# Half of wo and the FFN modulation weights in one transfer ahead of the last K, the other half behind the last V

## The chip, the cores and the metric

The kernel runs on one core of a Trainium2 chip. The metric is device time in microseconds (us), the median of a few runs. The profile is of one such execution; its span is the time from the first instruction to the last.

## The reference

One block of a decoder, for one token of each of 4 sequences: adaptive layer norm, attention over a cached window of 2048 positions with grouped heads, and a gated FFN. All data are fp32.

```python
mod = (_silu(c) @ w_mod).reshape(c.shape[0], 6, 1, -1)
sa, ca, ga, sb, cb, gb = (mod[:, 0], mod[:, 1], ..., mod[:, 5])
h = _layernorm(x, axis=-1) * (1 + ca) + sa
x = x + ga * _A_ref(h, A_k_cache, A_v_cache, A_wq, A_wo)   # attention, then @ wo
h = _layernorm(x, axis=-1) * (1 + cb) + sb
x = x + gb * _B_ref(h, B_w1, B_w3, B_w2)                   # (silu(h @ w1) * (h @ w3)) @ w2
return x
```

x is 4 x 512, there are 32 query heads on 8 key heads of 128 each, w_mod is 512 x 3072, wq 512 x 4096, wo 4096 x 512, w1 and w3 512 x 1792, w2 1792 x 512. Keys and values are by far the largest part: 8 MB for each of the 8 key heads (4 MB of K, 4 MB of V; MB and KB are powers of two wherever sizes of transfers are told, as in the profile's KB).

## The kernel before

**Memory.** One SBUF tensor, `ring`, holds three slots of 8 MB (64 KB on each of the 128 partitions); `HALF` is half a slot. Every large input is brought into a slot by a transfer that SP issues, in program order on one queue: `load(dst, src)` is one such transfer. In order: the attention part of w_mod (`w_mod_a`), x and c, wq, then K and V of groups 0 to 6 as one transfer of 8 MB each (`kv_in`), wo (8 MB), K of group 7 and V of group 7 apart (4 MB each), `w_mod_b` (the four FFN and gate parts of w_mod, 4 MB, with w1, 3.5 MB, in one transfer), w3 (3.5 MB), and w2 in four pieces (`W2_CUTS`: 8, 4, 1 and 1 fourteenths of 3.5 MB). In the profile all pieces of w1, w2 and w3 that have a transfer of their own are called `w`.

**Order.** The class `Program` records every operation in the order written, works out from the regions that operations touch which must wait for which, and puts a semaphore wait ahead of an instruction where its engine does not know already that the other is done. A transfer into a slot waits for the last matmul that reads what it overwrites. Each engine, SP among them, keeps the written order. Since all operations are issued in one helper line, all rows of the profile have the same line, and instructions are told apart by their tiles.

**Stages.** After the first norm, the query projection and the transposed queries (`qT`), `group(g)` runs for each of the 8 key heads: scores (`s_ps<-ring,qT`, 16 matmuls), the maximum on DVE (`mx`), the exponential on ACT (`p_sb`), transposed probabilities (`bank<-ident,p_sb`, then `pT`), and the product with V (`o_ps<-ring,pT`). ACT then scales the output into `o_sb`. `heads_out(g)` transposes it with the matrix `pick` into `oT`; it is called inside the next group, and for the last group after it. `project_out(g)` adds the product of this group's output and its rows of wo to `a_ps` (4 matmuls of width 512, tile `a_ps<-ring,oT`). Each fp32 matmul of the program gives two records in the trace.

wo arrives only between K of group 6 and K of group 7, so `project_out` is called for groups 0 to 5 just ahead of group 7, and for 6 and 7 after it. Then come `work` (a copy of `a_ps`), the product with `spread` that lays the attention output out over partitions (`attn`), `mod_columns` (16 matmuls `bank<-ring,sc` of width 512, from the activated c in `sc` and the FFN part of w_mod, copied to `mod_b`), the residual `x1`, the second norm, its transposition `h2T`, `ffn_in` for the gate (w1) and for up (w3) (`s_ps<-ring,h2T`), the hidden vector `hidT`, and the product with w2 (`s_ps<-ring,hidT`, 56 matmuls of width 128), gate, residual and the output.

Of the kernel before, what the change touches and what calls it, by code (L numbers as in the profile page):

```python
# [8 lines left out]
B, D, HQ, G, SK, DH, W, FF = 4, 512, 32, 8, 8192, 128, 2048, 1792  # L9
P = 128  # L10
R = HQ // G
# [1 line left out]
NC = 4  # L13
CHUNKS = [(c, j) for c in range(4) for j in range(4 if c < 2 else 3)]
NF = len(CHUNKS)
W2_CUTS = [0, 8, 12, 13, 14]
EPS = 1e-5
HALF = 8192

# [118 lines left out]
                nc.sync.sem_clear(done)  # L138


def block_kernel(nc, xc_in, w_mod_a, wq, kv_in, wo, w_mod_b, w3, w2, out):

# [1 line left out]
    do = Program(nc)  # L146

    def sb(name, *shape):
        return nc.alloc_sbuf_tensor(name, (P, *shape), F32).ap()

    def ps(name):
        return nc.alloc_psum_tensor(name, (P, 512), F32).ap()

    ring = sb("ring", 6 * HALF)
    slots = [ring[:, n * 2 * HALF : (n + 1) * 2 * HALF] for n in range(3)]
    s_ps = [ps(f"s_ps{t}") for t in range(NT)]
    banks = [ps(f"bank{n}") for n in range(2)]
    a_ps, o_ps = ps("a_ps"), ps("o_ps")
    turn = [0]

    def bank():
        turn[0] += 1
        return banks[turn[0] % 2]

    def load(dst, src):
        do("sync", "dma_start", dst, src)
        return dst

    def batch(t):

# [4 lines left out]
    x_sb, ct_sb = xc_sb[:, :P], xc_sb[:, P:]  # L175


    wma = load(slots[0][:, : w_mod_a.shape[1]], w_mod_a)
    load(xc_sb, xc_in)
    wq_t = load(slots[1], wq)  # L180
    kv = [None] * G
    kv[0] = load(slots[2], kv_in[0])
# [27 lines left out]
    oT = sb("oT", G, R, B)  # L210
# [9 lines left out]
    ss, ln, r0, ve, a, r = (sb(n, 1) for n in ("ss", "ln", "r0", "ve", "a", "r"))  # L220
# [26 lines left out]
    def mod_columns(wv, dst, n):  # L247

        pb = bank()
        for k in range(4):  # L250
            for j in range(4):
                do("tensor", "matmul", pb[32 * j : 32 * j + 32, : n * P], sc[:, k, :], wv[:, k, j, :], start=(k == 0), stop=(k == 3))
        do("vector", "tensor_copy", dst, pb[:, : n * P])
# [21 lines left out]
    for half in range(2):  # L275
# [4 lines left out]
        for i in range(R):  # L280
            src = qtp[:, i * P : (i + 1) * P].rearrange("p (g q) -> p g q", g=4)[:, :, ::8]
# [7 lines left out]

    def project_out(g):  # L290
        for i in range(R):
            do("tensor", "matmul", a_ps[32 * i : 32 * i + B, :], oT[:, g, i, :], wo_t[:, g, i, :], start=(g == 0), stop=(g == G - 1))

    mx, nm, ls, l, rl = (sb(n, m) for n, m in (("mx", NT), ("nm", 1), ("ls", NT), ("l", 1), ("rl", 1)))
    p_sb = [sb(f"p_sb{t}", 512) for t in range(NT)]
# [3 lines left out]
    def heads_out(g):  # L299

        otp = bank()[:, : R * B]
        for c in range(NC):
            do("tensor", "matmul", otp, o_sb[:, c * P : (c + 1) * P], pick[:, c].rearrange("p r b -> p (r b)"), start=(c == 0), stop=(c == NC - 1))
        do("vector", "tensor_copy", oT[:, g].rearrange("p r b -> p (r b)"), otp)

    def group(g):
        kt, vt = (kv[g][:, i * HALF : (i + 1) * HALF].rearrange("p (t b n) -> p t b n", t=NT, b=B) for i in range(2))
        for t in range(NT):
            for b in range(B):
                do("tensor", "matmul", s_ps[t][32 * b : 32 * b + 32, :], qT[:, g, b, :], kt[:, t, b, :], start=True, stop=True)  # L310
            do("vector", "reduce_max", mx[:, t : t + 1], s_ps[t], axis=AX.X)
        do("vector", "tensor_reduce", nm, mx, axis=AX.X, op=ALU.max, negate=True)
        if g:
            heads_out(g - 1)
        for t in range(NT):
            do("scalar", "activation", p_sb[t], s_ps[t], AF.Exp, bias=nm, accum_out=ls[:, t : t + 1])
            pt = bank()
            for c in range(NC):
                do("tensor", "transpose", pt[:, c * P : (c + 1) * P], p_sb[t][:, c * P : (c + 1) * P], ident)
            do("vector", "tensor_copy", pT[t], pt.rearrange("p (c b i) -> p b c i", b=B, i=32)[:, :, :, :R])  # L320
            for u in [t - 1] * (t > 0) + [t] * (t == NT - 1):
                for b in range(B):
                    do("tensor", "matmul", o_ps[32 * b : 32 * b + NC * R, :], pT[u][:, b].rearrange("p c r -> p (c r)"), vt[:, u, b, :], start=(u == 0), stop=(u == NT - 1))
        do("vector", "reduce_sum", l, ls, axis=AX.X)
        do("vector", "reciprocal", rl, l)
        do("scalar", "activation", o_sb, o_ps, AF.Copy, scale=rl)

    for g in range(G - 1):
        group(g)
        if g < 4:  # L330
            kv[g + 3] = load(slots[(g + 2) % 3], kv_in[g + 3])
        elif g == 4:
            wo_t = load(slots[0], wo).rearrange("p (g r n) -> p g r n", g=G, r=R)
        elif g == 5:
            kv[7] = slots[1]
            for i in range(2):
                load(kv[7][:, i * HALF : (i + 1) * HALF], kv_in[7][:, i * HALF : (i + 1) * HALF])
    wmb = load(slots[2][:, : w_mod_b.shape[1]], w_mod_b)
    for g in range(G - 2):
        project_out(g)  # L340
    group(G - 1)
    w3_t = load(slots[1][:, : w3.shape[1]], w3)
    w2_t = slots[1][:, HALF : HALF + w2.shape[1]]
    step = w2.shape[1] // NF
    for lo, hi in zip(W2_CUTS[:-1], W2_CUTS[1:]):
        load(w2_t[:, lo * step : hi * step], w2[:, lo * step : hi * step])
    project_out(G - 2)
    heads_out(G - 1)
    project_out(G - 1)

    do("scalar", "copy", work, a_ps)
    attn = bank()
    for j in range(4):
        do("tensor", "matmul", attn[32 * j : 32 * j + 32, :P], spread, work[:, j * P : (j + 1) * P], start=True, stop=True)

    mod_b = sb("mod_b", 512)
    ga, sh, cb1, gb = (mod_b[:, i * P : (i + 1) * P] for i in range(4))
    mod_columns(wmb[:, : 4 * 4 * 512].rearrange("p (k j i) -> p k j i", k=4, j=4), mod_b, 4)
    do("vector", "tensor_scalar_add", cb1, cb1, 1.0)
    x1, ag, tot2 = sb("x1", P), sq, sb("tot2", 1)  # L360
    do("vector", "tensor_mul", ag, attn[:, :P], ga)
    do("vector", "scalar_tensor_tensor", x1, ag, 1.0, x_sb, op0=ALU.mult, op1=ALU.add, accum_out=tot2)
# [4 lines left out]
    def ffn_in(ws, pg, g_sb):  # L367

        ws = ws.rearrange("p (k f) -> p k f", k=4)
        for k in range(4):
            for j in range(4):
                n = min(512, FF - 512 * j)
                do("tensor", "matmul", pg[32 * j : 32 * j + 32, :n], h2T[:, k, :], ws[:, k, j * 512 : j * 512 + n], start=(k == 0), stop=(k == 3))
        do("scalar", "copy", g_sb[:96], pg[:96])
        do("vector", "tensor_copy", g_sb[96:, :256], pg[96:, :256])
        gt = bank()
        for c in range(4):
            n, at = (128, c * 128) if c < 2 else (96, 256 + (c - 2) * 96)  # L380
            do("tensor", "transpose", gt[:, at : at + n], g_sb[:n, c * P : (c + 1) * P], ident[:n, :n])
        return gt[:, : NF * 32].rearrange("p (n i) -> p n i", i=32)[:, :, ::8]

    gate = ffn_in(wmb[:, 4 * 4 * 512 :], s_ps[0], p_sb[0])
    eg = sb("eg", NF, B)
    do("scalar", "activation", eg, gate, AF.Exp, scale=-1.0)
    do("vector", "tensor_scalar_add", eg, eg, 1.0)
# [6 lines left out]
    w2_t = w2_t.rearrange("p (n j i) -> p n j i", n=NF, j=4)  # L394
    for n in range(NF):
        if n == W2_CUTS[-2]:
            do.mark()
# [8 lines left out]
def _layout(i):  # L406
    import numpy as np

    def a(t):
        return np.ascontiguousarray(t)  # L410

    k = i["A_k_cache"][:, :, SK - W :, :].reshape(B, G, NT, 512, DH)
    v = i["A_v_cache"][:, :, SK - W :, :].reshape(B, G, NT, NC, P, DH)
    wm = i["w_mod"].reshape(4, P, 6, 4, P)
    xc = np.zeros((4, 32, P + 16), np.float32)
    xc[:, ::8, :P] = i["A_x"].reshape(B, 4, P).transpose(1, 0, 2)
    xc = xc.reshape(P, P + 16)
    xc[:, P:] = i["c"].reshape(B, 4, P).transpose(2, 1, 0).reshape(P, 16)
    w2 = i["B_w2"].reshape(14, P, D)
    w_mod_b = a(wm[:, :, 2:].transpose(1, 0, 3, 2, 4)).reshape(P, 8192)  # L420
    w1 = a(i["B_w1"].reshape(4, P, FF).transpose(1, 0, 2)).reshape(P, 4 * FF)
    return {
        "xc_in": xc,
        "w_mod_a": a(wm[:, :, :2].transpose(1, 0, 3, 2, 4)).reshape(P, 4096),
        "wq": a(i["A_wq"].reshape(4, P, G, 512).transpose(1, 2, 0, 3)).reshape(P, 16384),
        "kv_in": np.concatenate([k.transpose(1, 4, 2, 0, 3).reshape(G, P, 8192), v.transpose(1, 4, 2, 0, 3, 5).reshape(G, P, 8192)], 2),
        "wo": a(i["A_wo"].reshape(G, R, P, D).transpose(2, 0, 1, 3)).reshape(P, 16384),
        "w_mod_b": np.concatenate([w_mod_b, w1], 1),
        "w3": a(i["B_w3"].reshape(4, P, FF).transpose(1, 0, 2)).reshape(P, 4 * FF),
        "w2": a(np.stack([w2[4 * j + c] for c, j in CHUNKS], 1)).reshape(P, NF * D),  # L430
    }
# [15 lines left out]
```

## Time and profile before

| | us |
|---|---|
| median of 3 runs | 253.46 |
| lowest, highest | 251.55, 253.53 |
| the profiled execution | 253.12 |
| its span | 251.7 |
| PE busy | 154.6 (61%) |
| DVE busy | 47.5 (19%) |
| ACT busy | 33.4 (13%) |

The profiled execution moved 101.42 MB (here in millions of bytes) at a mean of 403 GB/s over its span. How to read the views that follow: a row of the timeline or the chain begins with a start time and a length in us, from the start of the span; "x32" counts instructions that stand together; brackets at a row's end give the idle time before it and what ended that. PEld is the load of a matmul's stationary operand, PE the matmul itself. A row of the table by stretches gives busy time by engine in the order PE, PEld, DVE, ACT, POOL, then the granted clock of PE as a share of full speed, the busy share of the transfer engines and GB/s. A transfer "lands" when its last byte is there and its semaphore counts full.

### The profile page before, as it was taken

How to read it: one execution, taken by the hardware profiler on the slowest of the kernel's cores; microseconds unless marked ns; L12 is line 12 of the kernel's file. 1: busy time of each engine (PE TensorE's matmuls, PEld its weight loads, DVE VectorE, ACT ScalarE, POOL GpSimd, SP SyncE). 2: the span in 40 equal slices, each digit the busy share in tenths (PEclk: the TensorE clock that was granted, in tenths of full speed). 3: DMA queues.
4: the chain of work that ended last, by engine and by line, in shares of the span. 5: the costliest groups of instructions: out<-in, count | busy, mean ns of one | idle time of the engine just before them, and what ended most of it. 6: DMA issues, size and time to landing. Idle time of an engine off the chain costs nothing.

```text
span 251.7 us, 2538 instructions
## 1 busy us (share of the span) xinstructions
PE 154.6 (61%) x1106; PEld 54.1 (21%) x1106; DVE 47.5 (19%) x155; ACT 33.4 (13%) x84; POOL 2.1 (1%) x9
## 2 busy tenths in 40 slices
PE   0340591279298489098298688278477768074975
PEld 0210130013033133023024124023111313011234
DVE  3220003041041041042032132023000500004021
ACT  2100000012004103104104104104100401000020
POOL 3000000000000000000000000000000000000000
PEclk9995589579867979869957979959959979757699
DMA  7999798998999989999899999999999999999700
GB/s 250 460 469 489 344 492 385 448 489 355 479 419 417 489 375 458 430 406 489 385 440 458 396 470 398 437 448 417 411 422 414 456 456 432 398 433 406 292 0 4
DMA packets 2778, 101.42 MB, mean 403 GB/s; under 512 B 320, under 2 KB 464, under 8 KB 720
## 3 DMA queue, kind: packets, MB, share of 16 engines
q1 hardware_dynamic: 2768, 101.27, 93.6%
q8 instruction: 8, 0.13, 0.2%
q14 instruction: 2, 0.02, 0.0%
HBM read 101.26 MB, written 0.01 MB: 402 GB/s over the span
## 4 chain that ended last, share of the span: by engine, by line
DMA 70%; PE 23%; DVE 3%; ACT 2%; issue 1%; SPq 0%; ACTq 0%; DVEq 0%
DMA ring<-kv_in 53%; DMA ring<-w_mod_b 17%; PE s_ps L52 12%; PE bank L52 7%; PE o_ps L52 5%; ACT p_sb L52 1%; DVE mx L52 1%; SPq L52 0%; DVE mod_b L52 0%; DVE p_sb L52 0%; DVE sq L52 0%; DVE nm L52 0%; DVE h L52 0%; DVE x L52 0%; DVE h2T L52 0%
## 5 line engine op out<-in xcount | busy, mean ns | idle before, releaser
L52 PE MATMUL s_ps<-ring,qT 128*32 128x512 f32 x256 | 44.6, 861 | 39.4 <-DMA ring<-kv_in 39.4
L52 DVE TENSOR_REDUCE mx<-s_ps 128x1 f32<-128x512 f32 x32 | 22.1, 692 | 89.4 <-PE s_ps L52 89.4
L52 PE MATMUL o_ps<-ring,pT 128*16 128x512 f32 x256 | 34.7, 639 | 2.9 <-DMA ring<-kv_in 2.9
L52 ACT ACTIVATE p_sb<-s_ps,nm 128x512 f32<-128x512 f32 x32 | 21.6, 686 | 101.2 <-PE bank L52 84.4
L52 PE MATMUL bank<-ident,p_sb 128*128 128x128 f32 (+1 forms) x136 | 23.8, 302 | 10.5 <-ACT p_sb L52 9.7
L52 PEld LDWEIGHTS s_ps<-ring,qT 128*32 128x32 f32 x256 | 10.1, 151 | 72.9 <-DMA ring<-kv_in 36.7
L52 PEld LDWEIGHTS bank<-ident,p_sb 128*128 128x128 f32 (+1 forms) x136 | 15.5, 150 | 31.7 <-ACT p_sb L52 14.2
L52 PE MATMUL s_ps<-ring,hT 128*32 128x512 f32 x64 | 9.3, 749 | 10.6 <-DMA ring<-wq 10.6
L52 DVE COPY pT<-bank 128x64 f32<-128x64 f32 x32 | 7.2, 225 | 44.2 <-PE bank L52 44.2
L52 PE MATMUL bank<-ring,sc 128*32 128x256 f32 (+1 forms) x64 | 10.0, 801 | 7.3 <-DMA ring<-w_mod_b 7.3
L52 PE MATMUL a_ps<-ring,oT 128*4 128x512 f32 x64 | 10.1, 778 | 5.6 <-DMA ring<-wo 5.3
L52 ACT ACTIVATE o_sb<-o_ps,rl 128x512 f32<-128x512 f32 x8 | 5.5, 688 | 43.3 <-PE o_ps L52 43.3
L52 PE MATMUL s_ps<-ring,h2T 128*32 128x512 f32 (+1 forms) x64 | 9.1, 662 | 0.4 <-DVE h2T L52 0.4
L52 PEld LDWEIGHTS bank<-pick,o_sb 128*128 128x128 f32 x64 | 7.7, 191 | 7.3 <-issue 6.3
L52 PE MATMUL bank<-pick,o_sb 128*128 128x16 f32 x64 | 8.5, 265 | 0.0
L52 PE MATMUL bank<-tot,avg 128*128 128x1 f32 x4 | 1.0, 312 | 11.5 <-DVE tot L52 9.9
L52 PEld LDWEIGHTS o_ps<-ring,pT 128*16 128x16 f32 x256 | 5.1, 96 | 12.5 <-issue 10.0
L52 ACT ACTIVATION_READ_ACCUMULATOR p_sb<-s_ps,nm 128x1 f32 x32 | 6.5, 203 | 0.0
L52 PEld LDWEIGHTS s_ps<-ring,hT 128*32 128x32 f32 x64 | 2.6, 135 | 16.7 <-issue 16.7
L52 DVE COPY qT<-bank 128x64 f32<-128x64 f32 x8 | 2.2, 276 | 20.6 <-PE bank L52 20.3
L52 PEld LDWEIGHTS bank<-ring,sc 128*32 128x32 f32 x64 | 2.8, 167 | 12.9 <-DMA ring<-w_mod_b 7.5
L52 ACT ACTIVATE work<-s_ps 128x512 f32<-128x512 f32 x2 | 1.2, 597 | 25.2 <-PE s_ps L52 21.8
(72 smaller groups left out, 42.3 us busy)
## 6 DMA issues: line engine op xcount, KB each, us to landing
ring<-kv_in SPq DMA_DIRECT2D x2, 4096.0 KB, 43.8
ring<-w_mod_b SPq DMA_DIRECT2D x1, 7680.0 KB, 42.8
ring<-w SPq DMA_DIRECT2D x1, 3584.0 KB, 32.6
ring<-w_mod_a SPq DMA_DIRECT2D x1, 2048.0 KB, 7.8
ring<-w SPq DMA_DIRECT2D x1, 2048.0 KB, 27.3
ring<-w SPq DMA_DIRECT2D x1, 1024.0 KB, 28.3
ring<-w SPq DMA_DIRECT2D x2, 256.0 KB, 28.2
ring<-kv_in SPq DMA_DIRECT2D x7, 44.4
```

The source lines that it names most:

```text
L52: op = Op(engine, lambda: getattr(getattr(self.nc, engine), method)(*args, **kw), [])
```

## The change

The 8 MB transfer ahead of the last K, until now all of wo, becomes `wo_mod`: the rows of wo of groups 0 to 3, and the FFN part of w_mod. The other half of wo follows the last V, into the lower half of slot 2, and w1 follows it as a transfer of its own, into the upper half. w3 comes in two halves and w2 in five pieces (6, 4, 2, 1 and 1 fourteenths), and both go into slot 0, whose contents are used ahead of group 7, instead of slot 1, which holds K and V of group 7. `project_out` is called for groups 0 to 3 ahead of group 7, and for 4 to 6 behind it. `mod_columns` with the addition to `cb1` moves ahead of group 7.

```diff
-W2_CUTS = [0, 8, 12, 13, 14]
+W2_CUTS = [0, 6, 10, 12, 13, 14]
+W3_CUTS = [0, 1, 2]
...
-    def load(dst, src):
-        do("sync", "dma_start", dst, src)
-        return dst
+    def load(dst, src, cuts=(0, 1)):
+        step = src.shape[1] // cuts[-1]
+        for lo, hi in zip(cuts[:-1], cuts[1:]):
+            do("sync", "dma_start", dst[:, lo * step : hi * step], src[:, lo * step : hi * step])
+        return dst[:, : src.shape[1]]
...
     def project_out(g):
         for i in range(R):
-            do("tensor", "matmul", a_ps[32 * i : 32 * i + B, :], oT[:, g, i, :], wo_t[:, g, i, :], start=(g == 0), stop=(g == G - 1))
+            do("tensor", "matmul", a_ps[32 * i : 32 * i + B, :], oT[:, g, i, :], wo_t[g // 4][:, g % 4, i, :], start=(g == 0), stop=(g == G - 1))
...
         elif g == 4:
-            wo_t = load(slots[0], wo).rearrange("p (g r n) -> p g r n", g=G, r=R)
+            wom = load(slots[0], wo_mod)
         elif g == 5:
+            load(slots[1], kv_in[7], (0, 1, 2))
             kv[7] = slots[1]
-            for i in range(2):
-                load(kv[7][:, i * HALF : (i + 1) * HALF], kv_in[7][:, i * HALF : (i + 1) * HALF])
-    wmb = load(slots[2][:, : w_mod_b.shape[1]], w_mod_b)
-    for g in range(G - 2):
+    wo_t = [t.rearrange("p (g r n) -> p g r n", g=4, r=R) for t in (wom[:, :HALF], load(slots[2][:, :HALF], wo))]
+    w1_t = load(slots[2][:, HALF:], w1)
+    for g in range(4):
         project_out(g)
+
+    mod_b = sb("mod_b", 512)
+    ga, sh, cb1, gb = (mod_b[:, i * P : (i + 1) * P] for i in range(4))
+    mod_columns(wom[:, HALF:].rearrange("p (k j i) -> p k j i", k=4, j=4), mod_b, 4)
+    do("vector", "tensor_scalar_add", cb1, cb1, 1.0)
     group(G - 1)
-    w3_t = load(slots[1][:, : w3.shape[1]], w3)
-    w2_t = slots[1][:, HALF : HALF + w2.shape[1]]
-    step = w2.shape[1] // NF
-    for lo, hi in zip(W2_CUTS[:-1], W2_CUTS[1:]):
-        load(w2_t[:, lo * step : hi * step], w2[:, lo * step : hi * step])
-    project_out(G - 2)
+    w3_t = load(slots[0][:, HALF:], w3, W3_CUTS)
+    w2_t = load(slots[0][:, :HALF], w2, W2_CUTS)
+    for g in range(4, G - 1):
+        project_out(g)
     heads_out(G - 1)
     project_out(G - 1)
...
-    mod_b = sb("mod_b", 512)
-    ga, sh, cb1, gb = (mod_b[:, i * P : (i + 1) * P] for i in range(4))
-    mod_columns(wmb[:, : 4 * 4 * 512].rearrange("p (k j i) -> p k j i", k=4, j=4), mod_b, 4)
-    do("vector", "tensor_scalar_add", cb1, cb1, 1.0)
...
-    gate = ffn_in(wmb[:, 4 * 4 * 512 :], s_ps[0], p_sb[0])
+    gate = ffn_in(w1_t, s_ps[0], p_sb[0])
```

The rest of the diff packs the inputs on the host accordingly.

Three places show what moves. The first is PE ahead of group 7: the last product with V of group 6, the products with wo, and the scores of group 7. Before:

```order
L52 MATMUL o_ps<-ring,pT 16x512 x8
L52 MATMUL a_ps<-ring,oT 4x512 x24
L52 MATMUL s_ps<-ring,qT 32x512 x16
L52 MATMUL bank<-pick,o_sb 128x16 x4
L52 MATMUL bank<-ident,p_sb 128x128 x8
```

After the change, the same place:

```order
L53 MATMUL o_ps<-ring,pT 16x512 x8
L53 MATMUL a_ps<-ring,oT 4x512 x16
L53 MATMUL bank<-ring,sc 32x512 x16
L53 MATMUL s_ps<-ring,qT 32x512 x16
L53 MATMUL bank<-pick,o_sb 128x16 x4
L53 MATMUL bank<-ident,p_sb 128x128 x8
```

Eight of the products with wo have left this place, and the 16 of the modulation columns have come in.

The second is PE behind group 7, from its last product with V to the transposed second norm. Before:

```order
L52 MATMUL o_ps<-ring,pT 16x512 x8
L52 MATMUL a_ps<-ring,oT 4x512 x4
L52 MATMUL bank<-pick,o_sb 128x16 x4
L52 MATMUL a_ps<-ring,oT 4x512 x4
L52 MATMUL bank<-work,spread 32x128 x4
L52 MATMUL bank<-ring,sc 32x512 x16
L52 MATMUL bank<-tot,avg 128x1
L52 MATMUL bank<-ss,avg 128x1
L52 MATMUL bank<-ident,h 128x128
```

After the change:

```order
L53 MATMUL o_ps<-ring,pT 16x512 x8
L53 MATMUL a_ps<-ring,oT 4x512 x12
L53 MATMUL bank<-pick,o_sb 128x16 x4
L53 MATMUL a_ps<-ring,oT 4x512 x4
L53 MATMUL bank<-work,spread 32x128 x4
L53 MATMUL bank<-tot,avg 128x1
L53 MATMUL bank<-ss,avg 128x1
L53 MATMUL bank<-ident,h 128x128
```

The modulation columns are gone from here, and the products of groups 4 and 5 with wo stand here with that of group 6.

The third is SP's queue of transfers, from wo on (width is in elements of 4 bytes on each partition). Before:

```order
L52 DMA ring<-wo 128x16384
L52 DMA ring<-kv_in 128x8192 x2
L52 DMA ring<-w_mod_b 128x15360
L52 DMA ring<-w 128x7168
L52 DMA ring<-w 128x4096
L52 DMA ring<-w 128x2048
L52 DMA ring<-w 128x512 x2
```

After the change:

```order
L53 DMA ring<-wo_mod 128x16384
L53 DMA ring<-kv_in 128x8192 x2
L53 DMA ring<-wo 128x8192
L53 DMA ring<-w 128x7168
L53 DMA ring<-w 128x3584 x2
L53 DMA ring<-w 128x3072
L53 DMA ring<-w 128x2048
L53 DMA ring<-w 128x1024
L53 DMA ring<-w 128x512 x2
```

The single transfer of w_mod and w1 has become w1 alone behind the second half of wo, and there are three transfers more.

More of the change, by code (lines that the diff above doesn't have):

```diff
@@ L138, in emit, with block_kernel @@
                 nc.sync.sem_clear(done)
-def block_kernel(nc, xc_in, w_mod_a, wq, kv_in, wo, w_mod_b, w3, w2, out):
+def block_kernel(nc, xc_in, w_mod_a, wq, kv_in, wo_mod, wo, w1, w3, w2, out):
     do = Program(nc)
@@ L175, in block_kernel @@
     x_sb, ct_sb = xc_sb[:, :P], xc_sb[:, P:]
-    wma = load(slots[0][:, : w_mod_a.shape[1]], w_mod_a)
+    wma = load(slots[0], w_mod_a)
     load(xc_sb, xc_in)
@@ L419, in _layout @@
     w2 = i["B_w2"].reshape(14, P, D)
-    w_mod_b = a(wm[:, :, 2:].transpose(1, 0, 3, 2, 4)).reshape(P, 8192)
-    w1 = a(i["B_w1"].reshape(4, P, FF).transpose(1, 0, 2)).reshape(P, 4 * FF)
+    wo = a(i["A_wo"].reshape(2, 4, R, P, D).transpose(0, 3, 1, 2, 4)).reshape(2, P, 8192)
     return {
@@ L426, in _layout @@
         "kv_in": np.concatenate([k.transpose(1, 4, 2, 0, 3).reshape(G, P, 8192), v.transpose(1, 4, 2, 0, 3, 5).reshape(G, P, 8192)], 2),
-        "wo": a(i["A_wo"].reshape(G, R, P, D).transpose(2, 0, 1, 3)).reshape(P, 16384),
-        "w_mod_b": np.concatenate([w_mod_b, w1], 1),
+        "wo_mod": np.concatenate([wo[0], a(wm[:, :, 2:].transpose(1, 0, 3, 2, 4)).reshape(P, 8192)], 1),
+        "wo": wo[1],
+        "w1": a(i["B_w1"].reshape(4, P, FF).transpose(1, 0, 2)).reshape(P, 4 * FF),
         "w3": a(i["B_w3"].reshape(4, P, FF).transpose(1, 0, 2)).reshape(P, 4 * FF),
```

## The prediction

> **What bounds the kernel now.** I read the page's account of the chain that ended last first: it says which work, followed back from the end, nothing else could have shortened.
>
> ```profile
> DMA 70%; PE 23%; DVE 3%; ACT 2%; issue 1%; SPq 0%; ACTq 0%; DVEq 0%
> ```
>
> Seventy per cent is transfers. The second view is the table by stretches, asked for one long stretch in the middle (after the busy times it gives the granted clock, the busy share of the transfer engines, and GB/s).
>
> ```profile
> 10.00:235.00 225.00, 142.18 (x931) 48.28 (x935) 41.94 (x129) 30.52 (x79) 0.00 (x0) 0.80 1.00 432
> ```
>
> The stream of transfers has no hole: share 1.00, 432 GB/s. So the time is the stream, plus what still has to be computed after the data that the tail needs. The third view, the chain piece by piece, shows that tail (start, length, what).
>
> ```profile
> 179.00 42.79 DMA ring<-w_mod_b
> ...
> 221.82 6.41 PE bank L52 x32
> ...
> 229.21 0.21 DVE sq L52
> ...
> 233.87 5.54 PE s_ps L52 x20
> ...
> 240.69 3.64 PE s_ps L52 x20
> ...
> 245.96 3.31 PE s_ps L52 x112
> ```
>
> The end hangs on the 7.5 MB transfer of w_mod and w1: lands at 221.8, then the modulation columns (6.4 us), the residual and the norm, gate at 233.87, up at 240.7, the w2 product at 245.96, the end of the span at 251.7. The attention output was ready long before: it waited from 214.6.
>
> When data land is read from the transfer queue: issue times from the timeline of SP, and us from issue to landing from the view of the transfers.
>
> ```profile
> 150.87 8.57 SPq L52 DMA_DIRECT2D ring<-kv_in  x2
> ring<-kv_in SPq DMA_DIRECT2D x1, 4096.0 KB, 43.1
> 159.12 0.33 SPq L52 DMA_DIRECT2D ring<-kv_in  x1
> ring<-kv_in SPq DMA_DIRECT2D x1, 4096.0 KB, 44.5
> 179.00 0.33 SPq L52 DMA_DIRECT2D ring<-w_mod_b  x1
> ring<-w_mod_b SPq DMA_DIRECT2D x1, 7680.0 KB, 42.8
> 197.65 0.33 SPq L52 DMA_DIRECT2D ring<-w  x1
> ring<-w SPq DMA_DIRECT2D x1, 3584.0 KB, 32.6
> 207.85 0.33 SPq L52 DMA_DIRECT2D ring<-w  x1
> ring<-w SPq DMA_DIRECT2D x1, 2048.0 KB, 27.3
> 210.59 0.43 SPq L52 DMA_DIRECT2D ring<-w  x1
> ring<-w SPq DMA_DIRECT2D x1, 256.0 KB, 28.4
> ```
>
> The last K lands at 150.87 + 43.1 = 194.0, the last V at 159.12 + 44.5 = 203.6, w_mod with w1 at 221.8, w3 at 230.3, the first w2 piece at 235.2, the last at 239.0. Transfers issued while others are in flight land one after the other, each after its own size: 4096 KB take 9.65 us (K to V), 7680 KB 18.2, 3584 KB 8.5, 2048 KB 4.9, and the last three pieces, 1536 KB, 3.8: 400 to 425 KB per us.
>
> **The change part by part.** It carries the same bytes, 15.5 MB between the sixth group's V and w3, in another order, so the stream should end where it did, at 239.0. No queue but SP's is touched; POOL has nothing there.
>
> *Issue.* The first transfer of the new pair waits for what wo waited for. The second half of wo waits only for the K reads of the group before the last, w1 for its V reads (179.0, as w_mod does now). w3 and w2 now wait for reads that stand ahead of the last group. Seven issues of 0.33 to 0.43 us follow at about 194; the stream has work until w1 lands at 221.8, so even 25 us of delay there opens no hole.
>
> *Landings.* Half of wo and w_mod land together where wo lands now, 184.2; K and V are unchanged; second half of wo 203.6 + 9.7 = 213.3; w1 221.8; w3's halves 226.0 and 230.3; w2's five pieces from 233.9 (1536 KB at 418 KB per us) to 239.0.
>
> *The columns ahead of the last group.* The timeline of PE (start, length, tile, count; in brackets the idle time before) and the weight loads beside it give the price. Every matmul of the program shows as two records.
>
> ```profile
> 184.27 8.05 PE L52 MATMUL a_ps<-ring,oT 128*4 128x512 f32 x48 [5.30 <-DMA ring<-wo]
> 193.98 3.64 PE L52 MATMUL s_ps<-ring,qT 128*32 128x512 f32 x32 [1.66 <-DMA ring<-kv_in]
> 185.08 0.15 PEld L52 LDWEIGHTS a_ps<-ring,oT 128*4 128x4 f32 x4 [0.70 <-issue]
> 185.94 0.15 PEld L52 LDWEIGHTS a_ps<-ring,oT 128*4 128x4 f32 x4 [0.71 <-issue]
> 190.43 0.10 PEld L52 LDWEIGHTS a_ps<-ring,oT 128*4 128x4 f32 x4 [0.33 <-issue]
> 190.86 0.10 PEld L52 LDWEIGHTS a_ps<-ring,oT 128*4 128x4 f32 x4 [0.33 <-issue]
> 184.27:189.80 5.53, 5.53 (x28) 1.00 (x32) 0.00 (x0) 0.00 (x0) 0.00 (x0) 0.50 1.03 441
> 189.80:192.30 2.50, 2.50 (x24) 0.39 (x16) 0.00 (x0) 0.00 (x0) 0.00 (x0) 1.00 1.02 433
> ```
>
> Four records step by 0.86 us at a granted clock of 0.50 and by 0.43 at 1.00: 0.213 and 0.107 us each. Ahead of the last group 48 records become 32 + 32 = 64. The 5.53 cold us take 26, the other 38 take 4.1: PE is free at 193.9, and K lands at 194.0. Cost nothing; the cover is K's landing. Were all 64 cold, 13.6 us, the scores would start at 197.9, 3.9 late; behind them stand a 2.85 us wait for V and the wait for wo below, 3.1, so even that costs nothing. DVE's copy and addition (1.0 us, the stretch from 228.2 to 229.2 in the chain) fall beside the first scores: DVE has nothing to reduce until their first 8 records are through, 0.9 us.
>
> *The new wait.* The last group ends as before, and then PE needs the second half of wo, for groups 4 to 6 (12 matmuls, 24 records). Queued behind it on PE are the last head's transposition and everything to the end; ACT and DVE wait for these.
>
> ```profile
> 203.77 1.91 PE L52 MATMUL o_ps<-ring,pT 128*16 128x512 f32 x8 [2.85 <-DMA ring<-kv_in]
> 208.29 1.91 PE L52 MATMUL o_ps<-ring,pT 128*16 128x512 f32 x16
> 211.06 1.07 PE L52 MATMUL bank<-pick,o_sb 128*128 128x16 f32 x8
> 212.40 1.04 PE L52 MATMUL a_ps<-ring,oT 128*4 128x512 f32 x8 [0.27 <-DVE oT L52]
> 214.14 0.43 PE L52 MATMUL bank<-work,spread 128*32 128x128 f32 x8 [0.71 <-ACT work L52]
> 203.77:206.86 3.09, 3.09 (x16) 1.00 (x20) 0.10 (x1) 0.00 (x0) 0.00 (x0) 0.50 0.87 378
> 206.86:210.30 3.44, 3.44 (x32) 1.00 (x28) 0.58 (x4) 0.00 (x0) 0.00 (x0) 1.00 0.99 429
> ```
>
> PE is done at 210.2, the data is there at 213.3, and PE starts 0.1 later (V: 203.6 and 203.77): 213.4. The 24 records cost between 2.6 (all at 1.00) and 5.1 us (all at 0.50). The nearest row is the wait for V: 2.85 us idle, then 3.1 us at 0.50, then 1.00. I take that: 3.1 us for 14.5 records, 1.0 for the rest, 4.1.
>
> *From there.* The last head's transposition to the end of the spread product takes 214.57 − 211.06 = 3.5 us, unchanged, and from the residual's multiplication to the first gate matmul 233.87 − 229.21 = 4.65; I add 0.1, since the chain shows only the end of that instruction. The columns (6.4), their copy and the wait of 7.2 us before them are gone from this place. Gate starts at 213.4 + 4.1 + 3.5 + 4.75 + 0.05 = **225.8** instead of 233.87: 8.1 us earlier. w1 has been there since 221.8.
>
> *What is late next.* Gate to end is 251.7 − 233.87 = 17.8, kept: **243.6**. Up starts 6.8 after gate, 232.6; w3 is whole at 230.3. The w2 product starts 12.1 after gate, 237.9; its last fourteenth is needed 3.0 later, 240.9, and lands at 239.0. So the stream is 1.9 us from being the bound; if it were, the end is 239.0 + 0.2 + 2.5 (from the product's end to the span's end) = 241.7. The finer pieces of w3 and w2 therefore buy nothing in this sum.
>
> *Sum.* The profiled execution took 253.12 us, 1.42 more than its span of 251.7. 243.6 + 1.4 = 245.0; that execution was 0.34 below the median of the runs shown (253.46), so between 245.0 and 245.4: I say **245.2**. The shortest run shown, 251.55, is 1.9 below the median, and nothing here explains it; it widens the range.
>
> Two rules of the Trainium skill bear on this. "TensorE: Matmul & The Clock Gate", in its part on the HAM clock gate, says that the clock drops after an idle window of about 3.4 us, and that this window runs free of the kernel. By it a wait of 3.1 us may or may not cool PE, from run to run; the trace agrees so far as 2.85 us of waiting was followed by 0.50. By the cold side the sum stands, by the warm one it is 1.5 lower, the second rival below. "DMA: Bandwidth & Descriptors", in the anatomy of one DMA, fits about 2.0 us of fixed cost per DMA on GpSimd's path, and its rules advise at least 1 MiB each: for three more transfers that is an estimated 6 us of stream, an end near 249. The trace differs: the pieces of this queue follow one another with no such hole.
>
> **The rivals.**
>
> *The wait leaves the clock at 1.00.* The 24 records cost 2.6, the gate starts at 224.3, the span is 242.1, the time 243.6. For it: PE is busy for 6.4 us ahead of the wait. Against it: the row at 203.77.
>
> *The tail runs cold.* The norm gives PE little to do. All of the 24 records, transposition, projection and spread at 0.50 add 1.0 + 1.1 + 1.0 + 0.4, and the gate matmuls, already mostly cold, some 0.5: 249. The warm row at 206.86 speaks against it.
>
> *Each extra transfer costs the stream.* Three more; it decides only above 1.9 / 3 = 0.6 us each. By the rows, SP's 0.43 us per issue as the most: 1.3, not enough, still 245; at 2 us each it is 249. Against it: 1536 KB in three pieces took 3.8 us.
>
> *Slower: transfers in flight share the engines.* Then the second half of wo, the largest of nine outstanding, lands not at 213.3 but towards 239, and the whole tail behind it follows: 239 + 12.4 + 17.8 = 269, about 271 as a time. It decides once that half lands after 221.4 (8.1 later), which is w1's place. Against it: K and V were in flight together and landed 9.65 us apart.
>
> *The change doesn't do what it says.* The columns on PE delay the last group by more than the two waits behind it absorb, 5.9 us: the gain shrinks by whatever is over. The sum finds 3.9 at the most; 250 or so if wrong.
>
> **How the numbers follow.** The forecast has 0.52, the warm clock 0.22, the cold tail 0.10, costly transfers 0.06, delayed columns 0.04, shared engines 0.03; 0.03 is left for what I don't see. A measurement of this kernel can tell about 1% (2.5 us) from no change. The first four cases are all faster by more, 0.90, and a part of the delayed columns with them: 0.91. Within 1%: 0.05. Slower: 0.04, sharing and a part of the rest. The range runs from 243.0 (warm clock and a little of the unexplained 1.9) to 248.5, which leaves out the extreme cold tail, the costly transfers and the slow cases.
>
> **What would show it.** In the changed profile: PE free of the columns within 0.5 us of the last K's landing; a PE wait of about 3 us for wo ahead of 24 a_ps records, ending near 213.4; these records in about 4 us; the gate near 226, with no wait for w1, w3 or w2; transfers ending at 239; wo instead of w_mod_b as the transfer in the chain. I am wrong if wo's second half lands far from 213, if the stream has a hole after 194, or if the w2 product waits for its last piece.

## The result, and the profile after

The changed kernel takes 244.06 us (median of 6 runs, 243.69 to 244.90) against 252.33 (6 runs, 251.10 to 253.53) for the kernel before: a ratio of 0.9675, 95% interval 0.9633 to 0.9716. That is 8.3 us less, as much as between the forecast 245.2 and the median of three runs known then (253.46), and 0.2 more than the sum's 8.1. Both times lie 1.1 us below those two, since the forecast was worked out from an execution of 253.12 us and the median of the kernel before came down with three more runs. The profiled execution took 244.61, its span is 243.2 us.

The page's account of the chain that ended last, by engine and by tile:

```profile
DMA 73%; PE 21%; DVE 2%; ACT 1%; issue 1%; SPq 1%; DVEq 0%; ACTq 0%
DMA ring<-kv_in 56%; DMA ring<-wo 18%; PE s_ps L53 12%; PE bank L53 4%; PE o_ps L53 3%; PE a_ps L53 2%; ACT p_sb L53 1%; SPq L53 1%; DVE mx L53 0%; DVE sq L53 0%; DVE p_sb L53 0%; ACT work L53 0%; DVE h L53 0%; DVE x L53 0%; DVE h2T L53 0%
```

The transfer that the end hangs on is now wo (its second half) instead of w_mod with w1. PE's timeline from there to the end (start, length, tile, count, and in brackets the idle time before):

```profile
184.24 5.82 PE L53 MATMUL a_ps<-ring,oT 128*4 128x512 f32 x32 [5.82 <-DMA ring<-wo_mod]
189.89 3.61 PE L53 MATMUL bank<-ring,sc 128*32 128x512 f32 x32
194.02 3.64 PE L53 MATMUL s_ps<-ring,qT 128*32 128x512 f32 x32 [0.53 <-DMA ring<-kv_in]
...
203.82 1.91 PE L53 MATMUL o_ps<-ring,pT 128*16 128x512 f32 x8 [2.90 <-DMA ring<-kv_in]
...
206.71 1.91 PE L53 MATMUL o_ps<-ring,pT 128*16 128x512 f32 x8
...
209.44 1.91 PE L53 MATMUL o_ps<-ring,pT 128*16 128x512 f32 x16
213.44 2.76 PE L53 MATMUL a_ps<-ring,oT 128*4 128x512 f32 x24 [2.09 <-DMA ring<-wo]
216.13 1.06 PE L53 MATMUL bank<-pick,o_sb 128*128 128x16 f32 x8
...
219.21 0.48 PE L53 MATMUL bank<-work,spread 128*32 128x128 f32 x8 [0.70 <-ACT work L53]
...
224.70 6.09 PE L53 MATMUL s_ps<-ring,h2T 128*32 128x512 f32 x32 [0.38 <-DVE h2T L53]
...
237.43 3.26 PE L53 MATMUL s_ps<-ring,hidT 128*32 128x128 f32 x112 [0.35 <-DVE hidT L53]
```

The columns (`bank<-ring,sc`) end at 193.5, and PE still waits 0.53 us for the last K: they cost nothing. The gate starts at 224.70 and not at 233.87, 9.2 us earlier; it waits for `h2T`, not for w1, and the w2 product waits for `hidT`, not for its data. The last transfer, from SP's timeline and the view of the transfers, lands at 195.80 + 43.4 = 239.2, as before (239.0):

```profile
195.80 7.24 SPq L53 DMA_DIRECT2D ring<-w  x1
```

```profile
ring<-w SPq DMA_DIRECT2D x1, 256.0 KB, 43.4
```

Three stretches of the table (after the busy times: granted clock, share of the transfer engines, GB/s) show what the sum had not foreseen in this execution:

```profile
213.44:216.20 2.76, 2.76 (x25) 0.61 (x25) 0.00 (x0) 0.00 (x0) 0.00 (x0) 1.00 1.04 447
219.45:222.86 3.41, 1.41 (x12) 1.00 (x4) 1.33 (x8) 0.47 (x2) 0.00 (x0) 0.50 0.93 395
224.70:229.69 4.99, 4.99 (x26) 1.35 (x29) 0.00 (x0) 0.00 (x0) 0.00 (x0) 0.50 1.00 424
```

The products behind the wait for wo ran at 1.00, and the norm and most of the gate at 0.50.

### The profile page after: what moved, and what is told of

Its sections match the earlier page's. It is cut to its first block, busy times and chain, and to the rows that moved or that the text cites. A ratio compares the mean times of both kernels' runs of the same rounds, so it can differ in the third digit from the quotient of the medians.

```text
span 243.2 us, 2543 instructions
## 1 busy us (share of the span) xinstructions
PE 152.1 (63%) x1106; PEld 54.2 (22%) x1106; DVE 47.6 (20%) x155; ACT 33.4 (14%) x84; POOL 2.1 (1%) x9
## 4 chain that ended last, share of the span: by engine, by line
DMA 73%; PE 21%; DVE 2%; ACT 1%; issue 1%; SPq 1%; DVEq 0%; ACTq 0%
DMA ring<-kv_in 56%; DMA ring<-wo 18%; PE s_ps L53 12%; PE bank L53 4%; PE o_ps L53 3%; PE a_ps L53 2%; ACT p_sb L53 1%; SPq L53 1%; DVE mx L53 0%; DVE sq L53 0%; DVE p_sb L53 0%; ACT work L53 0%; DVE h L53 0%; DVE x L53 0%; DVE h2T L53 0%
## 5 line engine op out<-in xcount | busy, mean ns | idle before, releaser
L53 PE MATMUL o_ps<-ring,pT 128*16 128x512 f32 x256 | 35.5, 653 | 2.9 <-DMA ring<-kv_in 2.9
L53 PE MATMUL s_ps<-ring,hT 128*32 128x512 f32 x64 | 8.8, 714 | 10.9 <-DMA ring<-wq 10.9
L53 PE MATMUL a_ps<-ring,oT 128*4 128x512 f32 x64 | 9.6, 745 | 8.2 <-DMA ring<-wo_mod 5.8
L53 PE MATMUL s_ps<-ring,h2T 128*32 128x512 f32 (+1 forms) x64 | 9.7, 700 | 0.4 <-DVE h2T L53 0.4
L53 PE MATMUL bank<-ring,sc 128*32 128x256 f32 (+1 forms) x64 | 7.0, 594 | 0.0
L53 PEld LDWEIGHTS a_ps<-ring,oT 128*4 128x4 f32 x64 | 1.6, 100 | 15.3 <-DMA ring<-wo_mod 6.7
```

Source lines behind the costliest of these rows:

```text
L53: op = Op(engine, lambda: getattr(getattr(self.nc, engine), method)(*args, **kw), [])
```

## The experiments

All kernels are changes to the changed kernel; each was timed beside the kernel before.

**The columns put back.** Same landings, but the modulation columns stand behind the spread product again.

```diff
@@ ahead of group 7
-    mod_columns(wom[:, HALF:].rearrange("p (k j i) -> p k j i", k=4, j=4), mod_b, 4)
-    do("vector", "tensor_scalar_add", cb1, cb1, 1.0)
     group(G - 1)
-    w3_t = load(slots[0][:, HALF:], w3, W3_CUTS)
-    w2_t = load(slots[0][:, :HALF], w2, W2_CUTS)
+    w3_t = load(slots[1][:, :HALF], w3, W3_CUTS)
+    w2_t = load(slots[1][:, HALF:], w2, W2_CUTS)
@@ behind the spread product
+    mod_columns(wom[:, HALF:].rearrange("p (k j i) -> p k j i", k=4, j=4), mod_b, 4)
+    do("vector", "tensor_scalar_add", cb1, cb1, 1.0)
```

> All transfers land in the order of the changed kernel, but the modulation columns stand on PE where they stood before the change, behind the spread product; w3 and w2 go into slot 1, as before the change, so that they don't wait for the columns. Theory (the gain has two parts: the landing order, and taking the columns off the path): the gate starts later by the columns, 3.5 to 6.4 us for 32 records, and their copy and addition, 1.0, so at 229 to 232 instead of 224.7, and the time is 248.5 to 251.5. Rival one (only the landing order counts, PE's place for the columns does not): 244 to 245. Rival two (the columns' place is the whole gain): 252.

Measured: 250.71 us (8 runs, 247.91 to 251.50), ratio 0.9911 (0.9874 to 0.9949). PE's timeline:

```profile
213.38 5.30 PE L53 MATMUL a_ps<-ring,oT 128*4 128x512 f32 x24 [4.57 <-DMA ring<-wo]
...
221.93 5.31 PE L53 MATMUL bank<-ring,sc 128*32 128x512 f32 x32
...
232.58 5.14 PE L53 MATMUL s_ps<-ring,h2T 128*32 128x512 f32 x32 [0.38 <-DVE h2T L53]
```

wo's half lands at the same time, but the columns (5.3 us) are back on the path and the gate starts at 232.6, 7.9 us later than in the changed kernel. Both single-cause rivals fall: with the landing order alone 0.9% is left, about 2.2 of 8.3 us; the rest needs the columns off the path. How the gain divides between the two hangs on the clock: behind a wait of 4.57 us the 24 records with wo took 5.30 us here instead of 2.76, which is 2.5 of the 7.9 us.

**w1 not apart.** wo's second half and w1 in one transfer.

```diff
-... load(slots[2][:, :HALF], wo))]
-    w1_t = load(slots[2][:, HALF:], w1)
+... load(slots[2], wo_w1)[:, :HALF])]
+    w1_t = slots[2][:, HALF : HALF + 4 * FF]
```

> One part undone: the second half of wo and w1 come as one transfer of 7.5 MB, which lands whole at 221.9 instead of wo's half at 213.4. Theory (everything behind the last group hangs on the landing of wo's second half): the 24 products with wo start 8.5 us later, the stream is unchanged, and the time is 252 to 253, all of the gain gone. Rival (the tail hangs on w1 or on the end of the stream, and wo's wait is only shown in front of it): 244 to 246.

Measured: 254.55 us (6 runs, 253.60 to 255.32), ratio 1.0082 (1.0046 to 1.0118).

```profile
221.75 5.29 PE L53 MATMUL a_ps<-ring,oT 128*4 128x512 f32 x24 [11.80 <-DMA ring<-wo_w]
```

Everything behind the last group hangs on that landing: it came 8.3 us later (213.44 to 221.75), and the span grew by 10.8 to 254.0. The 2.5 us by which the span grew more than the landing moved are in this row: behind a wait of 11.8 us the 24 records take 5.29 instead of 2.76. The time is 1.6 us above the expected stretch. So with this one part undone the change loses all of its gain and a little more.

**Many pieces.** w3 in 8 and w2 in 14 transfers.

```diff
-W2_CUTS = [0, 6, 10, 12, 13, 14]
-W3_CUTS = [0, 1, 2]
+W2_CUTS = list(range(15))
+W3_CUTS = list(range(9))
```

> w3 in 8 and w2 in 14 transfers, 15 more than in the changed kernel. Theory (a further transfer costs the stream nothing but what small pieces lose, 0.03 us each by the pieces of before): the stream ends by 239.8, the w2 product takes its last piece at 240.5, and the time stays at 243.7 to 245.0. Rival (a fixed cost of each transfer in the stream, 0.6 us or more): the stream ends 9 us later or more and sets the end, 252 or more; at 2 us each, 272.

Measured: 245.26 us (4 runs: 244.41, 244.44, 246.09, 246.15), ratio 0.9714 (0.9665 to 0.9763). PE's timeline, then SP's last two issues, and from the view of the transfers the last one's KB and us to landing:

```profile
213.31 4.44 PE L53 MATMUL a_ps<-ring,oT 128*4 128x512 f32 x24 [2.86 <-DMA ring<-wo]
...
238.99 3.26 PE L53 MATMUL s_ps<-ring,hidT 128*32 128x128 f32 x112 [0.35 <-DVE hidT L53]
```

```profile
229.99 1.10 SPq L53 DMA_DIRECT2D ring<-w  x2
```

```profile
ring<-w SPq DMA_DIRECT2D x1, 256.0 KB, 9.6
```

The last of 22 pieces is issued in the second half of SP's row (230.6) and lands at 240.2, 1.0 us later than in the changed kernel: 0.07 us for each of 15 further transfers, more than the 0.03 expected and far from 0.6 or 2. The product never waits for data. The median is above the expected stretch because the runs fall in two groups, 244.4 and 246.1; the profiled one belongs to the second, and its 24 records took 4.44 us; no profile shows a run of the first.

**w2 in two pieces**, `W2_CUTS = [0, 13, 14]`.

> w2 in two pieces, 13 and 1 fourteenths, so that the product's first matmul waits for nearly all of it. Theory (the stream is about 1 to 2 us from being the bound): the first piece lands at 238.5, the product starts there instead of at 237.4, and the time is 1.0 to 1.3 us above that of the changed kernel, 245.0 to 245.4. Rival (the pieces of w2 land well ahead of their use): no change, 244.1.

Measured: 245.55 us (4 runs, 245.41 to 245.66), ratio 0.9725 (0.9691 to 0.9759).

```profile
213.29 4.46 PE L53 MATMUL a_ps<-ring,oT 128*4 128x512 f32 x24 [3.18 <-DMA ring<-wo]
...
238.46 3.27 PE L53 MATMUL s_ps<-ring,hidT 128*32 128x128 f32 x112 [0.35 <-DVE hidT L53]
```

SP's row with the issue of the large piece (its second half), and from the view of the transfers that piece:

```profile
193.97 0.81 SPq L53 DMA_DIRECT2D ring<-w  x2
```

```profile
ring<-w SPq DMA_DIRECT2D x1, 3328.0 KB, 43.9
```

The time is near the expectation, but the profiled execution doesn't show the reason given: the product started late because of the clock behind wo, and waited for `hidT`, not for data. The piece landed only just ahead of it: issued at 194.3, it was there at 238.2, and the product started at 238.46. Where the changed kernel starts its product at 237.4, as in its first profile, this one would have to wait for the piece, so a faster clock behind wo could gain it some 0.2 us at most. That fits four runs within 0.25 us, none below 245.4, and so the theory; but no profile shows a run in which PE waits for the piece.

**The changed kernel again**, on the chip of the next three.

> The changed kernel itself, on the same chip as the three below. Expected: 243.7 to 245, spread over more than 1 us between runs, since the 24 products behind the wait for wo are run at a granted clock of 0.50 in some runs and of 1.00 in others.

Measured: 244.84 us (5 runs, 244.19 to 246.07), ratio 0.9717 (0.9689 to 0.9745). The profiled execution was again one with 2.76 us behind the wait:

```profile
213.47 2.76 PE L53 MATMUL a_ps<-ring,oT 128*4 128x512 f32 x24 [1.77 <-DMA ring<-wo]
```

The runs spread over 1.9 us, as expected, but the two clocks are not shown within this kernel's own profiles.

**wo in three**, and the last head's transposition ahead of the product of group 6.

```diff
-... load(slots[2][:, :HALF], wo))]
+... load(slots[2][:, :HALF], wo, (0, 2, 3, 4)))]
...
-    for g in range(4, G - 1):
+    for g in range(4, G - 2):
         project_out(g)
     heads_out(G - 1)
-    project_out(G - 1)
+    for g in range(G - 2, G):
+        project_out(g)
```

> The second half of wo in three transfers (groups 4 and 5 in 2 MB, 6 and 7 in 1 MB each), and the last head's transposition ahead of the product of group 6. Theory (the wait for wo's second half bounds the tail of the changed kernel, and the end of the stream is 1 to 2 us behind it as the next bound): the products of groups 4 and 5 need no wait, the spread product ends 2 to 4 us earlier, the w2 product is then paced by its last pieces, which land at 239.2, and the time is 243.2, 0.4 to 1.7 below the changed kernel, with runs closer together. Rival (a later wait, for w1 at 221.9 or a colder clock, takes the gain): 244 or more.

Measured: 243.81 us (4 runs, 243.62 to 244.00), ratio 0.9673 (0.9649 to 0.9697).

```profile
211.48 1.90 PE L53 MATMUL a_ps<-ring,oT 128*4 128x512 f32 x16
...
222.34 5.84 PE L53 MATMUL s_ps<-ring,h2T 128*32 128x512 f32 x32 [0.76 <-DMA ring<-w]
...
237.01 1.08 PE L53 MATMUL s_ps<-ring,hidT 128*32 128x128 f32 x32 [0.69 <-DMA ring<-w]
238.28 1.07 PE L53 MATMUL s_ps<-ring,hidT 128*32 128x128 f32 x24 [0.18 <-DMA ring<-w]
239.55 0.43 PE L53 MATMUL s_ps<-ring,hidT 128*32 128x128 f32 x8 [0.21 <-DMA ring<-w]
```

The wait for wo is gone, the gate waits 0.76 us for w1, and the w2 product waits for each of its last pieces: the stream is the bound. The span is 242.5. The time is 0.6 us above the expected 243.2 and 1.0 below the changed kernel beside it, with runs within 0.4 us; the two intervals of the ratio just overlap.

**The clock kept.** 14 unread matmuls between the steps of the second norm (2 ahead of the spread product, 3 and 3 ahead of the two sums, 6 ahead of the transposition).

```diff
+    def keep_warm(n):
+        for i in range(n):
+            do("tensor", "matmul", s_ps[3][:, :256], ident, o_sb[:, :256], start=True, stop=True)
```

> 14 further matmuls of width 256, whose result nobody reads, stand on PE between the steps of the second norm, where PE waits for DVE and ACT. Theory (the norm's waits cool PE, and the gate pays 2.5 us for it): the granted clock stays at 1.00 through the norm, the gate's 32 records take 3.6 us instead of 6.1, the w2 product becomes bound by its last pieces, and the time is 243.2 to 244.2. Rival (the clock is not what makes the gate slow, or the filling costs as much as it brings): 244.1 to 245.5.

Measured: 243.63 us (6 runs: 243.44, 243.51, 243.53, 243.72, 245.19, 245.23), ratio 0.9690 (0.9658 to 0.9721).

```profile
213.38 2.76 PE L53 MATMUL a_ps<-ring,oT 128*4 128x512 f32 x24 [2.32 <-DMA ring<-wo]
...
226.17 3.63 PE L53 MATMUL s_ps<-ring,h2T 128*32 128x512 f32 x32 [0.38 <-DVE h2T L53]
...
236.44 3.26 PE L53 MATMUL s_ps<-ring,hidT 128*32 128x128 f32 x112 [0.35 <-DVE hidT L53]
```

```profile
218.37:226.17 7.80, 7.42 (x45) 5.90 (x41) 2.47 (x12) 1.05 (x3) 0.00 (x0) 1.00 0.96 408
```

The clock stays at 1.00, the gate takes 3.63 us instead of the 6.09 and 6.50 of the changed kernel's two profiles, and the filling delays its start by 1.5 us. So it is the norm's waits that slowed the gate. The w2 product did not come to wait for its last pieces, as was expected; it runs unbroken behind `hidT`. Two runs at 245.2 stand apart from four at 243.4 to 243.7.

**Both.**

> wo in three and the kept clock together. Theory (the end of the stream is the bound for both, so they do not add): 243.2, as with wo in three alone. Rival (they add, the stream is not the bound): 241.5 or less.

Measured: 243.47 us (5 runs, 243.47 to 244.74), ratio 0.9678 (0.9651 to 0.9705).

```profile
230.54 1.92 PE L53 MATMUL s_ps<-ring,h2T 128*32 128x512 f32 x16 [0.83 <-DMA ring<-w]
...
239.25 0.43 PE L53 MATMUL s_ps<-ring,hidT 128*32 128x128 f32 x8 [0.21 <-DMA ring<-w]
```

They do not add. PE waits for the second half of w3 too, and the last chunk of the product starts when the last piece lands. Two runs took 244.5 and 244.7 with the same span as the others (242.2 against 242.1): what they have more lies ahead of the first or behind the last instruction, and no run shows what it is.

**The wait filled**: the kernel with the kept clock, and 6 such matmuls in the wait for wo's half.

> The kernel that keeps the clock through the norm, and 6 further unread matmuls of width 256 (1.6 us) on PE in the wait for wo's second half. The runs of the one without them fell at 243.5 and at 245.2 with nothing between. Theory (the two groups differ by the granted clock of the 24 products behind that wait): PE is idle for under 1.7 us there, the products run at 1.00 in every run, and all runs are at 243.3 to 243.9. Rival (the two groups come from elsewhere, the stream's start for one): again some runs near 245.2.

Measured: 243.92 us (6 runs, 243.55 to 244.34), ratio 0.9677 (0.9647 to 0.9707).

```profile
211.29 2.86 PE L53 MATMUL s_ps<-p_sb,ident 128*128 128x256 f32 x12
214.08 2.76 PE L53 MATMUL a_ps<-ring,oT 128*4 128x512 f32 x24
```

PE now has no idle time ahead of the 24 records, and no run near 245.2 is left, as expected; since only two of six were there before, six runs support this and don't prove it. The filling takes 2.86 us and not 1.6, so the products start 0.6 us late, and three runs lie up to 0.4 above the expected 243.9.

**The cuts as before**: `W2_CUTS = [0, 8, 12, 13, 14]`, `W3_CUTS = [0, 1]`.

> One part undone: w3 in one transfer and w2 in four pieces (8, 4, 1 and 1 fourteenths), as before the change; all else as changed. Theory (the finer pieces buy nothing): w3 lands at 230.5, needed at 232, the first piece of w2 at 235.4, needed at 237.4, and the time is that of the changed kernel, 244.0 to 244.9. Rival (the finer pieces carry a part of the gain): 245.5 or more.

Measured: 245.60 us (6 runs, 244.44 to 246.24), ratio 0.9731 (0.9692 to 0.9771).

```profile
213.43 4.46 PE L53 MATMUL a_ps<-ring,oT 128*4 128x512 f32 x24 [3.25 <-DMA ring<-wo]
...
238.50 3.26 PE L53 MATMUL s_ps<-ring,hidT 128*32 128x128 f32 x112 [0.35 <-DVE hidT L53]
```

The median is above the expected stretch, at the rival's edge. The profile speaks against the rival: neither up nor the w2 product waits for data, and the lateness is in the 24 records (4.46 us). The ratio's interval overlaps that of the changed kernel beside its own runs (0.9689 to 0.9745). The finer pieces bring nothing that these runs can tell.

## Why the prediction was right

- *Same stream, other order.* Right: the last transfer lands at 239.2 (239.0 forecast), wo's half lets PE start at 213.44 (213.4).
- *Columns ahead of the last group.* Right: PE is free at 193.5 (193.9 forecast), and K is still waited for. The first experiment prices what this takes off the path: 5.3 us of columns, and their copy behind them.
- *The new wait bounds the tail.* Right, and shown by the second experiment (the landing 8.3 us later, the span 10.8 longer) and by the sixth (the wait removed, the stream becomes the bound).
- *24 records in 4.1 us.* This term was mis-sized for this execution: 2.76. The wait was 2.09 us and not 3.1, since the last group's products ran longer at 0.50 (the eight records at 206.71 took 1.91 us, those of the kernel before 1.13) and ended at 211.35 and not at 210.2, and PE stayed at 1.00. Over the profiles, 2.76 stands behind idle times of 1.77 (the changed kernel again), 2.09 and 2.32 us, 4.44 and 4.46 behind 2.86, 3.18 and 3.25, and 5.3 behind 4.57 and 11.80. So a time near the forecast's 4.1 and one near its rival's 2.6 both occur, and both profiles of the changed kernel itself are the rival's.
- *Norm and gate unchanged.* Off by 0.2 (4.96 from the multiplication to the gate, 4.75 forecast) and 0.6 (12.73 from gate to the w2 product, 12.1): the gate ran colder, 6.09 against 5.45. The 24 records made the span 1.3 shorter than forecast, these two made it 0.8 longer, and 243.2 came out for a forecast 243.6: errors of the clock with opposite sign. That they nearly cancel is luck.
- *The stream 1.9 us from being the bound.* Right in kind: by the profile after it was 1.3 (243.2 against 239.2 + 0.2 + 2.5). Removing the wait brought 1.0 us against the changed kernel beside it, keeping the clock 1.2, and both together 1.4, not 2.2; these are differences of medians, and the intervals of the ratios overlap.
- *Seven issues at about 194.* Wrong, without consequence: the issues of w3 and w2 ran from 191.83 to 203.04, and one took 7.24 us. The stream had work meanwhile and ended where it was forecast.
- *Costs of transfers.* The fixed 2 us per DMA that the Trainium skill fits for GpSimd's path ("DMA: Bandwidth & Descriptors", the anatomy of one DMA) doesn't show on SP's queue: 0.07 us for each of 15 more.
- *The idle window.* The Trainium skill lets the clock drop after an idle window of about 3.4 us ("TensorE: Matmul & The Clock Gate", on the HAM clock gate). Here the 24 records already lost the full clock behind an idle time of 2.86 us (4.44 us instead of 2.76), and kept it behind 2.32; the measurement decides.

## What to carry to other kernels

Where transfers form one unbroken stream, the time is the stream plus what is computed behind the datum that lands latest for what it starts: order the landings by the length of the work behind each, and move work that needs only early data ahead of the last waits. Price the work behind a wait at both clocks: idle times up to 2.3 us left PE fast here, those from 2.9 us on were followed by half the clock for some time or throughout, and errors of this kind can cancel. Once the last pieces were waited for, shortening the tail further brought little: 1.4 us where 2.2 would have come by adding.

## What was not expected of the hardware

SP does not always issue in 0.33 to 0.43 us. With nine transfers outstanding (the last V, wo's half, w1, the halves of w3 and four pieces of w2) the tenth's issue took 7.24 us, from 195.80 to 203.04, about when the last V landed. The ninth, which found eight outstanding, had still taken 0.43. With w3 and w2 in 22 small pieces the issues were spread from 190 to 231; there too the first long ones, of 2.15 and 8.46 us, were those that found nine others outstanding, so pieces of 448 KB counted like a transfer of 4 MB. No run shows what sets the limit. It cost these kernels little, since the stream had work meanwhile: the w2 product waited for `hidT` in both.
